# The first sixty microseconds of a retention and GELU kernel: another order of transfers and units, and decay work moved between engines

## The chip, the cores and the metric

The kernel runs on one core of a Trainium2 chip. The metric is the device time of one execution in microseconds, from the first to the last instruction. The engines of a core run side by side, each in the order of its own queue, and wait for one another through semaphores: TensorE (PE in the profile, with its weight loads as PEld), VectorE (DVE), ScalarE (ACT), GpSimd (POOL), and SyncE (SP), which issues most of the transfers.

## The reference

The first part is a retention layer with a decaying state; the second is a feed-forward layer with the quick form of GELU. Everything is float32, but the two weight matrices are handed over as float64 and narrowed in the kernel.

```python
def _attn_ref(q, k, v):                      # (4, 8, 768, 64) each
    gamma = 1.0 - 2.0 ** (-5.0 - np.arange(H))
    scale = 1.0 / np.sqrt(D)
    for t in range(S):
        state = gamma * state + np.einsum('bhd,bhe->bhde', k[:, :, t], v[:, :, t])
        y[:, :, t] = scale * np.einsum('bhd,bhde->bhe', q[:, :, t], state)

def _moe_ref(x, w_in, w_out):                # x (3072, 512), w_in (512, 2048), w_out (2048, 512)
    h = x @ w_in
    g = h * (1.0 / (1.0 + np.exp(-1.702 * h)))
    return g @ w_out
```

Between the two, y is reordered to (B*S, H*D).

## The kernel before

The sequence is cut into 24 chunks: 64 time steps of two batches each. Four chunks make a block of 512 tokens, so there are six blocks. For a chunk j the kernel runs two functions:

- `turn(j)` transposes q and k on TensorE (blocks 0 and 1) into PSUM; ScalarE copies the result to SBUF. `decay(j)` scales k by the column decay.
- `attend(j, f)` makes the scores of chunk j, and, for the chunk f before it, the new state and the output: the product of the old state with q (scaled by the row decay, `rowd`) plus the product of v with the masked scores of f.

```python
    def turn(j):
        ...
            x = QKV.pop(("q", j)), QKV["kn", j]
            p = [ps.tile([P, 2, HP, D], F32, name="pt", tag="y") for i in range(2)]
            ...                      # 64 transposing matmuls against ident
            for i in range(2):
                act.activation(t[:, :, :, HALF[i]], p[i], AF.Copy)          # L229
            decay(j)
        ...
        if j + 2 < NCH and ...: load(j + 2, "qk")

    def decay(j):
        ...
        keep(pool.tensor_mul(KD[j], QKV.pop(("kn", j)), cold[...]))          # L244

    def attend(j, f=None):
        ...                          # scores L252; state L263; old state x q L272; v x scores L278
            dve.tensor_mul(AT[j], pa[:, :, 0], mask)                         # L282
        ...
            if c:
                dve.tensor_mul(tmp, py[:, :, 1]..., rowd...)                 # L293
                dve.tensor_add(x, y, tmp...)                                 # L295
            else:
                act.activation(x, y, AF.Copy)
            if c == 0:
                dve.tensor_copy(new, u)
            elif c < NC - 1:
                pool.tensor_mul(new, old, whole...)                          # L302
                dve.tensor_add(new, new, u)                                  # L303
            if f + 2 < 2 * CB: load(f + 2, "v")
```

`fetch()` issues the load of the next block (512 KB) of w_in, later of w_out, in its float64 form. `narrow()` makes float32 of what has been fetched: one ScalarE instruction and six of VectorE. The first two calls take one block each (together pair 0 of w_in's columns), every further call two blocks (a pair). There are 17 calls.

```python
        tc.keep_in_program_order(act.activation(m, hi, AF.Abs, scale=2.0 ** 16))      # L186
        tc.keep_in_program_order(dve.tensor_scalar(m, m, ..., op0=ALU.min, op1=ALU.max))  # L187
        dve.tensor_scalar(mu, mu, 3, None, op0=ALU.logical_shift_left)                # L189
        dve.scalar_tensor_tensor(hi, hi, 0x80000000, mu, ...)                         # L190
        dve.tensor_scalar(mu, hi, 0xFF800000, None, op0=ALU.bitwise_and)              # L191
        dve.scalar_tensor_tensor(lo, lo, 2.0 ** -52, m, ...)                          # L192
        dve.tensor_add(w, hi, lo)                                                     # L196
        for _ in range(n): fetch()
```

TensorE's order is the order of the text. For the other engines a scheduler orders the instructions when the program is built; `keep_in_program_order` pins an instruction behind the one that stands before it in the text on the same engine.

Block 0 of the feed-forward layer is computed in units `up0(half, p)`: eight matmuls of 256 columns for half of the block's tokens and pair p of w_in's columns, then a sigmoid and a product in `hidden`. Block 1 follows in units `up1(f)`. Then come `down(m)` for each block m, and `up(d)` for the blocks from 2 on; these use seven products of half-size matrices in place of eight, for which sums of w_out's parts (`sums_w2`, `sums_w2_t3`), of w_in's, of x's and of the hidden values (`sums_g`) are made. The start before:

```python
    load(0, "qk"); make_identity(nc, ident)
    ...                              # loads of cold, and of the row decay into m3, spread over 128 partitions
    fetch(); load(0, "v"); fetch(); load(1)
    ...                              # rowd copied out of m3; m3 times cold; selected to a triangle: mask
    keep_warm(7)                     # 7 transposes of ident
    narrow()
    turn(0)
    ...                              # load of whole
    attend(0)
    narrow()
    for _ in range(2): fetch()
    turn(1)
    attend(1, 0)
    for _ in range(2): fetch()
    turn(2)
    for j in range(2, 5):
        attend(j, j - 1)
        turn(j + 1)
        narrow()
        up0(0, j - 2, "x")
    between = [...]                  # (attend(5, 4), turn(6)), (attend(6, 5), turn(7)), attend(7, 6), attend(None, 7)
    for n, unit in enumerate([(1, p) for p in range(3)] + [(half, p) for p in range(3, NP) for half in range(2)]):
        up0(*unit, "xxyx"[n % 4])
        if n % 2 == 0: narrow()
        if n in (1, 4, 7, 10): between.pop(0)()
    for f in range(NFF):
        up1(f)
        if f % 2 == 0: narrow()
        if f >= NFF - 4: sums_w2(2 * (f - NFF + 4))
    ...
        for n, unit in enumerate(down(m)):
            unit()
            if m == 0 and n < NP // 2: sums_w2_t3(2 * n)
```

## Time and profile before

| what | value |
|---|---|
| time, median of three runs | 691.2 us (690.55 to 695.37) |
| span of the profiled run | 692.5 us |
| matmuls of block 0 (`up0`), first and last start | 32.3 and 106.3 us |
| matmuls of block 1 (`up1`), first start | 113.75 us |
| first unit of `down(0)` | 168.8 us |
| moved by the transfers, whole span | 46.85 MB, 68 GB/s |
| moved between 10 and 60 us | 207 to 220 GB/s in each 10 us |

A line of a timeline gives the start in us, the length in us, the engine, the line of the kernel, the operation, the tile written and the tiles read, the shape, the count, and in brackets the idle time of the engine before it and what ended it. A float32 matmul of the text appears as two instructions in the trace. Consecutive matmuls overlap in the profile, so that the time of a group is read from the starts, not from the sum of the single times.

### The profile page before, as it was taken

What the parts mean: (1) busy time and instruction counts of PE and PEld (TensorE: products, weight loads), DVE (VectorE), ACT (ScalarE), POOL (GpSimd) and SP (SyncE); (2) the same over time, 40 slices, a digit from 0 to 9 for tenths busy, and PEclk for the clock granted to TensorE, in tenths of its full rate; (3) what the DMA queues carried; (4) which work ended last, traced back from release to release, by engine and by line L of the source; (5) the groups of instructions that cost most, each with busy time, mean ns of one, the idle gap of its engine ahead of it and who ended that gap; (6) DMA issues with size and microseconds to landing.
All of it is one profiled execution on the core that took longest, in us unless ns stands there. A gap on an engine that the chain in (4) does not pass through costs nothing.

```text
span 692.5 us, 14320 instructions
## 1 busy us (share of the span) xinstructions
PE 670.6 (97%) x6087; PEld 562.0 (81%) x6087; DVE 368.7 (53%) x512; ACT 127.7 (18%) x201; POOL 145.2 (21%) x131
## 2 busy tenths in 40 slices
PE   5779999999999999999999999999999999999997
PEld 4668886445888888888888888888888888888886
DVE  3499999997341563344373445373345373344241
ACT  3232323331000000332000333000233000233000
POOL 4221200000168343100244100244200143000030
PEclk9999999999999999999999999999999999999999
DMA  8875544422212213310323320223320220000001
GB/s 199 220 194 169 160 147 137 168 50 32 41 20 57 66 29 76 74 36 4 68 36 87 74 43 2 58 48 88 74 42 1 45 50 31 17 0 1 16 0 46
DMA packets 140368, 46.85 MB, mean 68 GB/s; under 512 B 131792, under 2 KB 132816, under 8 KB 140304
## 3 DMA queue, kind: packets, MB, share of 16 engines
q1 hardware_dynamic: 136352, 39.10, 24.6%
q0 software_dynamic: 1808, 5.52, 2.2%
q10 hardware_dynamic: 2144, 1.31, 0.6%
q8 instruction: 48, 0.79, 0.5%
q14 instruction: 16, 0.13, 0.1%
HBM read 39.59 MB, written 6.29 MB: 66 GB/s over the span
## 4 chain that ended last, share of the span: by engine, by line
PE 84%; DVE 11%; DMA 3%; issue 1%; POOL 0%; ACT 0%; ACTq 0%; SPq 0%; POOLq 0%
PE pd L439 39%; PE px L386 16%; PE py L386 12%; PE ph L347 8%; PE ph L334 3%; DMA kn_in<-in_k_dram 3%; PE pa L252 2%; PE py L278 1%; PE py L272 1%; DVE W L196 1%; PE pa L263 1%; DMA whole<-in_col_decay_dram 1%; DVE W L189 1%; DVE W L192 1%; DVE W L191 1%
## 5 line engine op out<-in xcount | busy, mean ns | idle before, releaser
L439 PE MATMUL pd<-W,G 128*128 128x256 f32 x1120 | 247.4, 381 | 0.4 <-DVE G L377 0.3
L439 PEld LDWEIGHTS pd<-W,G 128*128 128x128 f32 x1120 | 211.3, 190 | 30.3 <-DVE G L377 1.2
L386 PE MATMUL px<-X,W 128*128 128x256 f32 x512 | 119.0, 379 | 0.0
L386 PEld LDWEIGHTS px<-X,W 128*128 128x128 f32 x512 | 97.3, 190 | 13.2
L386 PE MATMUL py<-X,W 128*128 128x256 f32 x384 | 90.7, 379 | 0.0
L386 PEld LDWEIGHTS py<-X,W 128*128 128x128 f32 x384 | 73.0, 190 | 9.9
L334 PE MATMUL ph<-X,W 128*128 128x256 f32 x256 | 59.8, 394 | 5.9 <-DVE W L196 5.3
L334 PEld LDWEIGHTS ph<-X,W 128*128 128x128 f32 x256 | 50.0, 198 | 13.7 <-DVE W L196 5.5
L244 POOL TENSOR_TENSOR kd<-kn_in,cold 128x512 f32<-128x512 f32 x14 | 17.2, 1225 | 188.1 <-PE pa L263 161.3
L347 PE MATMUL ph<-W,W 128*128 128x512 f32 x128 | 55.2, 593 | 0.3 <-DVE W L315 0.3
L347 PEld LDWEIGHTS ph<-W,W 128*128 128x128 f32 x128 | 24.2, 190 | 30.8 <-issue 29.7
L378 POOL TENSOR_TENSOR G<-G 128x512 f32<-128x512 f32 x20 | 29.5, 1482 | 91.9 <-DVE G L377 90.4
L282 DVE TENSOR_TENSOR at<-pa,mask 128x512 f32<-128x512 f32 x16 | 11.0, 686 | 62.1 <-PE pa L263 53.6
L315 DVE TENSOR_TENSOR G<-G,sg 128x512 f32<-128x512 f32 x48 | 33.0, 688 | 14.0 <-ACT sg L313 14.0
L431 POOL DMA_DIRECT2D out_dram<-o x20 | 14.9, 746 | 121.2 <-DVE o L430 121.2
L313 ACT ACTIVATE sg<-G 128x512 f32<-128x512 f32 x48 | 30.2, 630 | 51.3 <-DVE G L396 30.7
L439 PE MATMUL pd<-W,W 128*128 128x256 f32 x160 | 35.8, 381 | 0.4 <-DVE W L377 0.3
L302 POOL TENSOR_TENSOR state<-state,whole 128x512 f32<-128x512 f32 x20 | 22.0, 1098 | 66.0 <-DVE state L303 60.5
L313 ACT ACTIVATE sg<-ph 128x512 f32<-128x512 f32 x32 | 19.1, 598 | 88.4 <-PE ph L334 40.8
L439 PEld LDWEIGHTS pd<-W,W 128*128 128x128 f32 x160 | 30.2, 190 | 5.6 <-DVE W L377 1.2
L396 DVE TENSOR_TENSOR G<-py,p 128x512 f32<-128x512 f32 x16 | 11.1, 692 | 37.8 <-PE py L386 37.8
L426 ACT ACTIVATE u<-pd 128x512 f32<-128x512 f32 x6 | 3.6, 597 | 135.6 <-PE pd L439 135.6
(105 smaller groups left out, 659.0 us busy)
## 6 DMA issues: line engine op xcount, KB each, us to landing
W<-in_moe_w_in_dram SPq DMA_DIRECT2D x12, 512.0 KB, 5.6
v_in<-in_v_dram SPq DMA_DIRECT2D x48, 128.0 KB, 3.3
kn_in<-in_k_dram SPq DMA_DIRECT2D x42, 128.0 KB, 3.2
W<-in_moe_w_out_dram SPq DMA_DIRECT2D x10, 512.0 KB, 4.1
out_dram<-o POOLq DMA_DIRECT2D x20, 256.0 KB, 2.7
q_sq<-in_q_dram SPq DMA_DIRECT2D x256, 16.0 KB, 1.9
k_sq<-in_k_dram SPq DMA_DIRECT2D x256, 16.0 KB, 1.8
G<-in_moe_w_out_dram SPq DMA_DIRECT2D x6, 512.0 KB, 5.1
```

The source lines that it names most:

```text
L244: keep(pool.tensor_mul(KD[j], QKV.pop(("kn", j)), cold[:, H:2 * H, None].to_broadcast([P, H, D])))
L252: pe.matmul(pa[HALF[i], r, 0, s, :], KT[j][HALF[r], s, HALF[i]], QT[j][HALF[r], s, HALF[i]], start=True, stop=True)
L302: pool.tensor_mul(new, old, whole[:, None, :, None].to_broadcast([P, 2, HP, D]))
L313: act.activation(s, h, AF.Sigmoid, scale=1.702)
L315: dve.tensor_mul(g, h[:, i], s[:, i])
L334: pe.matmul(h[:, ab], w, X[:, 2 * half + c // 2, c % 2, :], start=(ab == 0 and c == 0), stop=(c == 3), skip_group_check=True)
L347: pe.matmul(h, w, X1[:, c // 2:4:2, c % 2, :], start=(c == 0), stop=(c == 3))
L378: pool.tensor_sub(a[1], a[1], a[0])
L386: pe.matmul(acc[:, u, :], W1[:, 2 * d + u, sa, c, :], X[:, sb, c, :], start=(start and u == 0 and c == 0), stop=(stop and c == 1), skip_gr ...
L396: dve.tensor_add(a[0], y, p1)
L431: (pool if m < NB - 1 else act).dma_start(rows[th, e], o)
L439: pe.matmul(p0[:, n, :], g1(m, p, sa)[:, n * P:(n + 1) * P], W2[:, sb, p, :], start=(new and p == 0 and n == 0), stop=(last and p == NP - ...
```

## The change

- **Transfers.** q, k and v of chunk 0 are issued ahead of w_in's first blocks; four blocks are fetched ahead of the units. The row decay is loaded as one row of one partition and spread by a matmul against a row of ones (`rows`).
- **Row decay in q's turn.** In chunks 1 to 7, q is transposed against a diagonal that holds the row decay (`diag`), so that the scores and the product with the old state carry it already. The mask then needs the column decay only. Chunk 0 is turned against the identity, and its output is multiplied by the row decay. For the later chunks the mask gets its row decay during `up1`.
- **ScalarE takes work of blocks 0 and 1.** k's decay becomes eight activations with a scale per partition, the state's decay four; the product with `rowd` becomes a plain copy on ScalarE. Before, GpSimd and VectorE did these.
- **Units.** The first unit of block 0 comes as soon as chunks 0 and 1 are done; the turns of chunks 2 and 3 follow between units. `keep_warm` uses matmuls on quarters of the array in place of transposes, and is called in four places.
- **w_out's sums** move from the end of `up1` to the first product groups of `down(0)`, and the last of them from the first group to the third.

```diff
@@ turn
-                pe.matmul(p[i][HALF[r], n, s, :], x[n][HALF[i], HP * r + s, :], ident[HALF[i], HALF[i]],
+                pe.matmul(p[i][HALF[r], n, s, :], x[n][HALF[i], HP * r + s, :],
+                          ident[HALF[i], HALF[i]] if n or j == 0 else diag[HALF[i], HP * r + s, :],
                           start=True, stop=True)
...
-            decay(j)
+            if j:
+                decay(j)
@@ decay
-        keep(pool.tensor_mul(KD[j], QKV.pop(("kn", j)), cold[:, H:2 * H, None].to_broadcast([P, H, D])))
+        x, d = QKV.pop(("kn", j)), cold[:, H:2 * H, None]
+        if j < 2 * CB:
+            for h in range(H):
+                tc.keep_in_program_order(act.activation(KD[j][:, h], x[:, h], AF.Copy, scale=d[:, h]))
+        else:
+            pool.tensor_mul(KD[j], x, d.to_broadcast([P, H, D]))
@@ attend
+            if c == 0 and f:
+                act.activation(x, y, AF.Copy)
+            elif c == 0:
+                dve.tensor_mul(x, y, rowd[:, :, None, :].to_broadcast([P, HP, 2, D]))
+            else:
+                if f < 2 * CB:
+                    act.activation(tmp, z, AF.Copy)
+                else:
+                    dve.tensor_mul(tmp, z, scale)
                 dve.tensor_add(x, y, tmp.rearrange(by, t=D))
...
-                pool.tensor_mul(new, old, whole[:, None, :, None].to_broadcast([P, 2, HP, D]))
+                if f < 2 * CB:
+                    for s in range(HP):
+                        tc.keep_in_program_order(act.activation(new[:, :, s], old[:, :, s], AF.Copy, scale=whole[:, s:s + 1]))
+                else:
+                    pool.tensor_mul(new, old, whole[:, None, :, None].to_broadcast([P, 2, HP, D]))
                 dve.tensor_add(new, new, u)
@@ start
-    load(0, "qk")
+    load(0, "q")
+    load(0, "k")
+    load(0, "v")
...                                  # cold and row loaded, mask from cold alone
     fetch()
-    load(0, "v")
     fetch()
     load(1)
+    fetch()
+    fetch()
...
-    keep_warm(7)
+    keep_warm(9)
+    turn(0)
+    rd = rows("x")
     narrow()
-    turn(0)
+    attend(0)
...                                  # rowd and diag copied from rd; decay(0); diag selected to a diagonal; whole loaded
-    attend(0)
+    keep_warm(12)
     narrow()
-    for _ in range(2):
-        fetch()
     turn(1)
+    keep_warm(4)
     attend(1, 0)
-    for _ in range(2):
-        fetch()
+    fetch()
+    fetch()
+    keep_warm(4)
+    attend(None, 1)
+    narrow()
+    up0(0, 0, "x")
     turn(2)
-    for j in range(2, 5):
-        attend(j, j - 1)
-        turn(j + 1)
-        narrow()
-        up0(0, j - 2, "x")
-    between = [lambda j=j: (attend(j, j - 1), turn(j + 1)) for j in (5, 6)] + [lambda: attend(7, 6), lambda: attend(None, 7)]
+    up0(0, 1, "x")
+    attend(2)
+    turn(3)
+    narrow()
+    up0(0, 2, "x")
+    attend(3, 2)
+    attend(None, 3)
+    narrow()
+    between = [lambda: turn(4), lambda: (attend(4), turn(5)), lambda: (attend(5, 4), turn(6)),
+               lambda: (attend(6, 5), turn(7)), lambda: attend(7, 6), lambda: attend(None, 7)]
...
-        if n % 2 == 0:
+        if n % 2 == 0 and n < 12:
             narrow()
-        if n in (1, 4, 7, 10):
+        if n in (1, 2, 4, 6, 8, 10):
             between.pop(0)()
@@ up1, down
-        if f >= NFF - 4:
-            sums_w2(2 * (f - NFF + 4))
+        if f == 1:
+            dve.tensor_mul(m3, m3, rows("x"))
...
-            if m == 0 and n < NP // 2:
-                sums_w2_t3(2 * n)
+            if m == 0 and n < NP and n % 2:
+                sums_w2(n - 1)
+            if m == 0 and NP <= n < 3 * NP // 2:
+                sums_w2_t3(2 * (n - NP))
```

More of the change, by code (lines that the diff above doesn't have):

```diff
@@ L96 @@
     rowd = const.tile([P, HP, D], F32, name="rowd")
+    row = G[0:1, 4, 0:2].rearrange("p a (h t) -> p (a h) t", t=D)
+    ones = G[0:1, 4, 2, 0:P]
     cold = const.tile([P, 2 * H], F32, name="cold")
@@ L121, in load @@
                 plain("q", q, "q_sq", 2)
+            if "k" in what:
                 plain("kn", k, "k_sq", 2, sp if j else act)
@@ L242, in decay @@
         KD[j] = home(j, "kd")
-        keep = tc.keep_in_program_order if j == 0 else lambda i: i
-        keep(pool.tensor_mul(KD[j], QKV.pop(("kn", j)), cold[:, H:2 * H, None].to_broadcast([P, H, D])))
+        x, d = QKV.pop(("kn", j)), cold[:, H:2 * H, None]
[4 more added lines that the diff above has]
+            pool.tensor_mul(KD[j], x, d.to_broadcast([P, H, D]))
     def attend(j, f=None):
@@ L289, in attend @@
             by = "p i r (s t) -> p (r s) i t"
-            y = py[:, :, 0].rearrange(by, t=D)
-            if c:
-                tmp = two.tile([P, 2, 2, P], F32, name="tmp", bufs=1)
-                dve.tensor_mul(tmp, py[:, :, 1].rearrange("p r i t -> p i r t"),
-                               rowd.rearrange("p (r s) t -> p r (s t)", r=2)[:, None].to_broadcast([P, 2, 2, P]))
+            y, z = py[:, :, 0].rearrange(by, t=D), py[:, :, 1].rearrange("p r i t -> p i r t")
+            scale = rowd.rearrange("p (r s) t -> p r (s t)", r=2)[:, None].to_broadcast([P, 2, 2, P])
+            tmp = two.tile([P, 2, 2, P], F32, name="tmp", bufs=1)
+            if c == 0 and f:
[7 more added lines that the diff above has]
+                    dve.tensor_mul(tmp, z, scale)
                 dve.tensor_add(x, y, tmp.rearrange(by, t=D))
-            else:
-                act.activation(x, y, AF.Copy)
             u = pa[:, :, 1]
@@ L468, in down @@
         return todo
-    load(0, "qk")
+    load(0, "q")
+    load(0, "k")
+    load(0, "v")
+    W = col_decay.shape[1]
+    for i in range(2):
+        tc.keep_in_program_order(pool.dma_start(
+            cold[HALF[i]].rearrange("p (n h) -> p n h", n=2),
+            bass.AP(tensor=col_decay.tensor, offset=col_decay.offset, ap=[[W, D], [D * W + H, 2], [1, H]])))
+    tc.keep_in_program_order(pool.dma_start(row, row_decay[None, :, 0:D]))
     make_identity(nc, ident)
-    W = col_decay.shape[1]
+    dve.memset(ones, 1.0)
     m3 = mask.rearrange("p r h t -> p (r h) t")
-    for i in range(2):
-        pool.dma_start(cold[HALF[i]].rearrange("p (n h) -> p n h", n=2),
-                       bass.AP(tensor=col_decay.tensor, offset=col_decay.offset, ap=[[W, D], [D * W + H, 2], [1, H]]))
-    pool.dma_start(m3, bass.AP(tensor=row_decay.tensor, offset=row_decay.offset, ap=[[0, P], [P, H], [1, D]]))
     first = const.tile([P, 1], F32, name="first")
@@ L484, with rows @@
     fetch()
-    load(0, "v")
     fetch()
     load(1)
-    idle = ps.tile([P, HP, P], F32, name="idle", tag="x")
+    fetch()
+    fetch()
+    idle = ps.tile([P, 4 * P], F32, name="idle", tag="x")
     def keep_warm(n):
         for _ in range(n):
-            pe.transpose(idle[:, 0, :], ident, ident)
-    for o in range(2):
-        act.activation(rowd[HALF[o]], m3[HALF[o], o:H:2, :], AF.Copy)
-    dve.tensor_mul(m3, m3, cold[:, 0:H, None].to_broadcast([P, H, D]))
+            for h in HALF:
+                pe.matmul(idle[h, 0:P], ident[h, h], ident[h, :], start=True, stop=True)
+    def rows(tag):
+        p = ps.tile([P, H, D], F32, name="rows", tag=tag)
+        pe.matmul(p.rearrange("p h t -> p (h t)"), ones, row.rearrange("p h t -> p (h t)"), start=True, stop=True)
+        return p
+    dve.tensor_copy(m3, cold[:, 0:H, None].to_broadcast([P, H, D]))
     for i in range(2):
-        pool.affine_select(out=m3[HALF[i]], in_=m3[HALF[i]], compare_op=ALU.is_ge, fill=0.0, base=0,
-                           pattern=[[0, H], [1, D]], channel_multiplier=-1)
+        tc.keep_in_program_order(pool.affine_select(
+            out=m3[HALF[i]], in_=m3[HALF[i]], compare_op=ALU.is_ge, fill=0.0, base=0,
+            pattern=[[0, H], [1, D]], channel_multiplier=-1))
+    diag = one.tile([P, H, D], F32, name="diag", tag="kT")
     def chunks(first, last):
@@ L507, in chunks @@
                 for s in (lambda j=j: turn(j), lambda j=j: attend(j, j - 1))]
-    keep_warm(7)
+    keep_warm(9)
+    turn(0)
+    rd = rows("x")
     narrow()
-    turn(0)
+    attend(0)
+    for o in range(2):
+        act.activation(rowd[HALF[o]], rd[HALF[o], o:H:2, :], AF.Copy)
+    act.activation(diag, rd, AF.Copy)
+    decay(0)
+    for i in range(2):
+        tc.keep_in_program_order(pool.affine_select(
+            out=diag[HALF[i]], in_=diag[HALF[i]], compare_op=ALU.is_equal, fill=0.0, base=0,
+            pattern=[[0, H], [1, D]], channel_multiplier=-1))
     for r in range(2):
```

## The prediction

> **What bounds the kernel now.** I read the page first: the busy times and the span in 40 slices.

> ```profile
> span 692.5 us, 14320 instructions
> PE 670.6 (97%) x6087; PEld 562.0 (81%) x6087; DVE 368.7 (53%) x512; ACT 127.7 (18%) x201; POOL 145.2 (21%) x131
> PE   5779999999999999999999999999999999999997
> DVE  3499999997341563344373445373345373344241
> ```

> TensorE (PE) is busy for 670.6 of 692.5 us, so only 21.9 us are idle. The slices say where: the first three, and the last. The stretches view adds up the idle time of PE from 0 to 60 us as 16.5 us, and from 600 us to the end as 4.1 us; in between there are 1.3 us. VectorE (DVE) is as full as PE from slice 3 to slice 9, though only 53% busy over the whole. So a change of the order of work can win something only before about 55 us, and must not push DVE over its limit between 35 and 125 us.

> Next I read the list of waits from 0 to 230 us, for PE.

> ```profile
> PE ph L334 <- DVE W L196: 5.3, 2, 3.4
> PE pa L252 <- ACT G L229: 3.9, 3, 2.8
> PE pt L224 <- DMA q_in<-in_q_dram: 2.9, 2, 2.3
> PE idle L493 <- POOL ident masks.py:199: 2.6, 1, 2.6
> PE pt L224 <- DMA kn_in<-in_k_dram: 1.6, 1, 1.6
> ```

> Columns: total us, times, longest. The waits are of three kinds: for a narrowed block of w_in (L196 is the last DVE instruction of `narrow`), for the copies of the transposed q and k, and for loads. Then the timelines of PE and ScalarE (ACT), first 65 us:

> ```profile
> 30.12 1.06 PE L224 MATMUL pt<-ident,q_in 64*64 64x64 f32 x30 [2.26 <-DMA q_in<-in_q_dram]
> 32.33 4.95 PE L334 MATMUL ph<-X,W 128*128 128x256 f32 x16
> 42.29 3.72 PE L334 MATMUL ph<-X,W 128*128 128x256 f32 x16 [1.88 <-DVE W L196]
> 52.37 9.92 PE L334 MATMUL ph<-X,W 128*128 128x256 f32 x38 [3.39 <-DVE W L196]
> 68.09 10.63 PE L334 MATMUL ph<-X,W 128*128 128x256 f32 x48 [0.68 <-ACT G L229]
> ...
> 32.32 1.08 ACT L229 ACTIVATE G<-pt 128x512 f32<-128x512 f32 x2 [8.19 <-PE pt L224]
> 33.29 1.12 ACT L186 ACTIVATE W<-W 128x1024 f32<-128x1024 f32 x1
> ```

> The three `up0` units of the loop start at 32.33, 42.29 and 52.37 us; **from 52.37 us on PE stands still for no more than 0.7 us at a time** until the tail. The 48 matmuls from 68.09 took 221 ns each, a unit of 16 so 3.54 us. The three units from 52.37 to 64.38 took 12.0 instead of 10.6 us: 1.4 us lost to a lower clock after the 3.39 us wait. The first unit waits for chunk 3's transposes (q lands at 30.1), although it needs only chunks 0 and 1. The two ACT lines show that the `Abs` of a narrow is pinned behind the instruction traced before it: its two blocks of w_in were issued by 19.9 us and no block took over 9.1 us to land, so the pin held it, not the data.

> [...] 1.4 us lost after 3.39 us idle, nothing visible after 1.88 us. [...] Here L189 took 1.42 us beside GpSimd's k decay at 45.2 us and 0.69 at 55.3. [...] here 128x512 from SBUF took 0.67 us and 128x1024 1.15, so about 0.19 us fixed and 0.94 ns per element.

> **The change part by part.**

> (1) Start. The mask needs the column decay only (4 KB a transfer) and no 256 KB row decay, which landed at 10.6 and held ACT and the mask until 13.9. K's second half landed at 8.65 and still sets the end of `turn(0)`, say 9.5. The `Abs` of the first narrow runs about 10.0 to 10.6, 0.9 us earlier than now. From there DVE has no pause: two half narrows of 3.45 us each (0.45+0.45+0.7+0.45+0.7+0.7, the unblocked durations less overlap), two masks, x(0), state, x(1), state at 0.6: 10.5. So DVE is through chunk 1 at about 10.6+10.5 = 21 if nothing is late; the chain through PE and ACT gives 22.4: row decay copies (2 x 0.41), diag 0.6, k's decay in eight strips of 0.19+64x0.00094 = 0.25, together 2.0; the diag's two selects of 0.84 on GpSimd let turn(1) begin at about 13.8; turn 1.0, copies 1.1, attend(1, 0) 2 with the clock up, warm-up 0.9, the last attend 1.5, tmp 0.6, four strips of state at 0.31, add 0.6. **The first unit can start at about 21.5 instead of 32.33.**

> (2) What follows it. The narrow of pair 1 has its `Abs` pinned behind the state strips, so L187 starts at 23.0. A pair costs 0.7+0.7+1.23+0.68+1.23+1.22 = 5.76 us; with one gated product (0.6) in it, pair 1 is ready at 29.4. Unit (0,1) runs 29.4 to 33.0, attend(2) and turn(3) to 34.4, copies to 35.4, k's strips to 37.4, `Abs` to 38.5, pair 2 to 44.3. Unit (0,2) now stands directly behind its own narrow: PE waits from 34.4 to 44.3, goes cold, and needs 3.54+1.7 = 5.2 us, to 49.5. attend(3, 2) to 51.4; tmp, strips, add 2.4; the last attend 0.9, tmp and x 1.2: **unit (1,0) starts at 55.9 and PE is dense from there.**

> (3) Work done by then. Against 52.37 before: one unit more (3.54), turns 4 and 5 (0.94 each) and the scores of chunk 4 (0.5) not yet done: 1.15 us ahead. Equivalent 54.75, against 52.37 plus the 1.4 lost to the clock, 53.8: +1.0 us. To this come the second `rows` product in the dense stretch, 512 columns wide as in L347, where a product is two instructions of 0.43 us: 0.86, and turn(5) right behind a unit that holds a "y" buffer, whose release takes a sigmoid and a product, less 0.5 for the scores between: about 0.7. **Sum +2.6 us.**

> (4) DVE later. Seven tmp products leave (7 x 0.6 = 4.2 us), the twelve subtractions of w_out's sums (12 x 0.6 = 7.2) leave the `up1` stage, and blocks by GpSimd end in chunks 0 to 7. None of it is on the path: PE was dense there. After: the sums have the 14 us of the first two products of `down(0)`, which read slices 0 and 2 of w_out alone. The t3 subtractions (4 x 0.6) fall beside sums_g, where PE waited 0.29 us at 196.3; DVE was idle for 8.45 us before 180, and will probably do them early. Worth: 0.

> **Rivals.** A, the sum above: the wait for the narrows only moves, from 42 and 52 to 29 and 34 us. For it: the pins, and DVE's 5.76 us a pair, which nothing shortens. It gives 691.2+2.6 = 693.8. B: the whole chain starts earlier than I put it, since q, k and v now stand ahead of w_in's blocks in the queue (k, 2 us earlier), the strips overlap on ACT (1 us each in the two chains that count, 2 us), turn(5) finds its buffer (0.7), and the third unit's wait is filled or short enough for the clock to stay up (1.7). Against A that is 6.4: 687.4. For it: ACT's two copies from PSUM take 1.08 where one takes 0.6, so they overlap, and the warm-up counts (12 and 4) look like values tuned against this very gap. Against it: rowd's two copies did not overlap (0.84 for two of 0.41). C: the loads bound it. The stretches show 207 to 220 GB/s between 10 and 60 us; by unit (0,1) q and k of chunks 0 to 2, v of 0 and 1 and four to six blocks of w_in are needed, 4.2 to 5.2 MB, that is 20 to 25 us at 210 GB/s, less than the 29.4 of DVE. If GpSimd's later transfers or a full queue delay them, 4 us more than A: 697.8.

> **Range and chances.** A takes the late end of nearly every estimate, so I weigh A 0.3, B 0.6 and C 0.1: 0.3x693.8 + 0.6x687.4 + 0.1x697.8 = 690.4. I put **690.0 us**, a range of 684.0 to 696.0. Two per cent is 13.8 us, near the whole idle time before 55 us, so faster by that has 0.06, slower 0.03, within 0.91.

> **What would show it.** Unit (0,0) at 20 to 23 us; PE idle before (0,1) and, longest of all, 8 to 10 us before (0,2), ended by the last instruction of a narrow; a granted clock below 1 in the slice after; from (1,0) on no wait over 1.5 us; DVE below 98% between 60 and 125 us; no GpSimd decay before `down(0)`; the end of `up1` within 3 us of 169. I am wrong if the third unit starts before 40 us (then B and more), if a load ends PE's waits after 20 us (C), or if the time from the first `down` unit to the end is not the old 523.7 us within 1 us.

## The result: the change makes the kernel slower, and the profile after

| kernel | median us | before, same chip | ratio with 95% interval |
|---|---|---|---|
| after | 709.87 (709.66 to 711.66) | 691.36 | 1.0259 [1.0223, 1.0296] |

The prediction was 690.0 us with a range up to 696.0: it was wrong. All rivals named in it lay below 698 us as well.

The first part of the page of the kernel after: busy times, two engines in 40 slices, and the clock granted to TensorE.

```profile
span 708.0 us, 14607 instructions
PE 675.6 (95%) x6200; PEld 564.6 (80%) x6200; DVE 364.2 (51%) x508; ACT 154.4 (22%) x300; POOL 127.6 (18%) x118
PE   7647999999999999999999999999999999999997
DVE  3634988799671183344383344383344383344241
PEclk9967999999999999999999999999999999999999
```

Where the kernel before had "577" in PE's first three slices and nines from the fourth, there is now "7647". A slice is 17.7 us, so the third and fourth are 35 to 71 us: there PE is less busy, and its clock is down to six and seven tenths. From the fifth slice on PE is full again. The loss lies in the stretch that was to become shorter.

The list of waits of the kernel after, first 230 us, PE alone (total us, times, longest):

```profile
PE ph L354 <- DVE W L199: 12.9, 2, 10.1
PE idle L519 <- POOL ident masks.py:199: 3.9, 1, 3.9
PE ph L354 <- DVE X L313: 2.9, 2, 1.4
PE pa L274 <- issue: 2.6, 1, 2.6
PE py L289 <- issue: 1.7, 1, 1.7
```

L354 is the matmul of `up0`, L199 the last VectorE instruction of `narrow` (L334 and L196 before). The wait for the narrows grew from 5.3 to 12.9 us, 10.1 of it in one piece. No load stands in these lines any more; before, q and k made up 4.5 us. "issue" in the last two lines is PE standing still without a releaser that the list knows; it comes up again below.

PE's timeline of the kernel after. In order: the units (0,0), (0,1), (0,2), the last scores and state of chunk 3, the units (1,0) and (1,1), and the first `up1`.

```profile
24.34 1.56 PE L354 MATMUL ph<-X,W 128*128 128x256 f32 x6 [1.44 <-DVE X L313]
...
32.40 5.38 PE L354 MATMUL ph<-X,W 128*128 128x256 f32 x16 [2.81 <-DVE W L199]
...
49.42 5.95 PE L354 MATMUL ph<-X,W 128*128 128x256 f32 x16 [10.09 <-DVE W L199]
...
60.04 0.69 PE L274 MATMUL pa<-v_in,G 64*64 64x64 f32 x32 [2.65 <-issue]
63.72 9.09 PE L354 MATMUL ph<-X,W 128*128 128x256 f32 x32 [1.42 <-DVE X L313]
...
127.64 7.13 PE L367 MATMUL ph<-W,W 128*128 128x512 f32 x16 [1.37 <-DVE W L335]
```

The first unit starts 8 us earlier than before (24.34 against 32.33), as intended, and (0,1) and (0,2) still start earlier than they did (42.29 and 52.37 before). The fourth, (1,0), is late: the point from which PE is dense came at 52.37 us before and comes at 63.72 now, with 1.15 us of work more done. `up1` starts at 127.64 against 113.75, 13.9 us late; `down(0)` starts at 183.92 against 168.79, 15.1 late; and from there to the end of the span it is 524.1 us against 523.7. That makes 15.5 us between the two spans, not 18.5: the profiled execution of the kernel before took 694.2 us, 2.8 more than its median.

What stands behind the wait of 10.09 us: the timelines of ScalarE and then of VectorE in the kernel after.

```profile
39.42 1.08 ACT L234 ACTIVATE G<-pt 128x512 f32<-128x512 f32 x2 [1.02 <-PE pt L228]
40.40 2.01 ACT L253 ACTIVATE G<-kn_in,cold 128x64 f32<-128x64 f32 x8
42.30 1.10 ACT L189 ACTIVATE W<-G 128x1024 f32<-128x1024 f32 x1
```

```profile
43.44 0.69 DVE L190 TENSOR_SCALAR W<-W 128x1024 f32<-128x1024 f32 x1 [3.71 <-ACT W L189]
...
48.14 1.23 DVE L199 TENSOR_TENSOR W<-G 128x1024 f32<-128x1024 f32 x1
```

ScalarE copies the turned q and k of chunk 3, then scales k in eight strips (2.01 us), and only then does the `Abs` (L189) that opens the narrow of pair 2. VectorE had nothing to do for 3.71 us, then works 5.9 us on the pair while PE stands still.

### The profile page after: what moved, and what is told of

The parts are those of the page before. It is cut to its first block, busy times and chain, and to the rows that moved or that the text cites. A ratio compares the mean times of both kernels' runs of the same rounds, so it can differ in the third digit from the quotient of the medians.

```text
span 708.0 us, 14607 instructions
## 1 busy us (share of the span) xinstructions
PE 675.6 (95%) x6200; PEld 564.6 (80%) x6200; DVE 364.2 (51%) x508; ACT 154.4 (22%) x300; POOL 127.6 (18%) x118
## 4 chain that ended last, share of the span: by engine, by line
PE 89%; DVE 7%; ACT 2%; issue 2%; POOL 0%; ACTq 0%; POOLq 0%
PE pd L459 39%; PE px L406 16%; PE py L406 12%; PE ph L367 8%; PE ph L354 6%; PE pa L263 2%; PE py L289 2%; PE py L283 1%; PE pa L274 1%; PE pt L228 1%; PE idle L519 1%; ACT W L189 1%; DVE W L199 1%; DVE G L396 1%; DVE W L396 1%
## 5 line engine op out<-in xcount | busy, mean ns | idle before, releaser
L354 PE MATMUL ph<-X,W 128*128 128x256 f32 x256 | 63.9, 410 | 16.7 <-DVE W L199 12.9
L354 PEld LDWEIGHTS ph<-X,W 128*128 128x128 f32 x256 | 51.9, 206 | 25.7 <-DVE W L199 10.2
L398 POOL TENSOR_TENSOR G<-G 128x512 f32<-128x512 f32 x20 | 29.5, 1482 | 91.8 <-DVE G L397 91.8
L322 POOL TENSOR_TENSOR state<-state,whole 128x512 f32<-128x512 f32 x13 | 14.3, 1098 | 122.0 <-DVE state L323 121.7
```

The lines of the kernel that those rows point to most:

```text
L322: pool.tensor_mul(new, old, whole[:, None, :, None].to_broadcast([P, 2, HP, D]))
L354: pe.matmul(h[:, ab], w, X[:, 2 * half + c // 2, c % 2, :], start=(ab == 0 and c == 0), stop=(c == 3), skip_group_check=True)
L398: pool.tensor_sub(a[1], a[1], a[0])
```

## The experiments

My theory after the comparison: the order of the text ties the narrow of pair 2 behind `turn(3)` and its strips, and the units right behind it; the wait and the cold clock after it (0.50 from 43.74 to 53.98 us) are the loss, and ScalarE's strips make it longer. Its rival: not the order but the other parts (transfers, row decay, work on ScalarE) are the loss. A third theory, that PE waits for its own instructions, came up with e4. The quoted expectations were each written before their run, and some give the theories letters: O is the order, S ScalarE's strips, F the wait for instructions.

All medians are in us; "over" is the difference to the median of the kernel before on the same chip.

| run | median | before | over | ratio with 95% interval |
|---|---|---|---|---|
| after | 709.87 | 691.36 | +18.5 | 1.0259 [1.0223, 1.0296] |
| e1: decays back on GpSimd | 701.98 | 693.17 | +8.8 | 1.0114 [1.0037, 1.0192] |
| e2: narrow of pair 2 early | 697.80 | 693.17 | +4.6 | 1.0058 [1.0037, 1.0080] |
| e3: before, new order of units only | 714.84 | 693.17 | +21.7 | 1.0297 [1.0233, 1.0361] |
| e4: after, old order of units | 711.92 | 693.17 | +18.8 | 1.0247 [1.0181, 1.0313] |
| e5: e4, eight warm-up rounds more | 705.14 | 692.99 | +12.2 | 1.0171 [1.0117, 1.0224] |
| e6: e1 and e2 together | 696.47 | 692.99 | +3.5 | 1.0053 [1.0035, 1.0071] |
| e7: before, sums moved only | 694.21 | 692.99 | +1.2 | 1.0008 [0.9986, 1.0030] |
| e8: e5 with decays on GpSimd | 701.39 | 692.99 | +8.4 | 1.0125 [1.0069, 1.0182] |
| e9: before, narrow a line up | 693.14 | 694.39 | -1.3 | 0.9985 [0.9965, 1.0006] |
| e10: e9, unit ahead of the turn too | 694.26 | 694.39 | -0.1 | 0.9998 [0.9982, 1.0015] |
| e11: before, 48 idle matmuls more | 699.84 | 694.39 | +5.5 | 1.0070 [1.0047, 1.0094] |
| e12: e3 with narrow of pair 2 early | 705.55 | 694.39 | +11.2 | 1.0133 [1.0079, 1.0186] |
| e13: after, warm-up ahead of (0,2) | 710.40 | 693.67 | +16.7 | 1.0253 [1.0190, 1.0315] |
| e14: before, new transfers only | 697.36 | 693.67 | +3.7 | 1.0054 [1.0036, 1.0073] |

In the first row the kernel before has the median of four executions, in the others of 23 to 55 on other chips; against those medians 709.87 is 15.5 to 16.9 us over.

### e2: the narrow one step earlier

```diff
     up0(0, 0, "x")
+    narrow()
     turn(2)
     up0(0, 1, "x")
     attend(2)
     turn(3)
-    narrow()
     up0(0, 2, "x")
```

> The changed kernel with one line moved: the narrow of pair 2 is traced directly behind the first unit, not behind turn(3). Theory O: VectorE goes from pair 1 to pair 2 without its pause of 11 us; pair 2 is ready near 38.5 us instead of 49.4, the third unit starts near 40 us, the clock stays up, unit (1,0) starts near 52 instead of 63.7 us, and the time falls by 11 to 14 us, to 696 to 699. Theory S: the strips still stand in the chain; under 4 us gained, about 707.

This moves one line. The `Abs` of pair 2 is now pinned ahead of the copies and strips of chunks 2 and 3. PE's timeline of this kernel, units (0,1), (0,2) and (1,0):

```profile
33.07 5.16 PE L354 MATMUL ph<-X,W 128*128 128x256 f32 x16 [3.67 <-DVE W L199]
39.72 3.72 PE L354 MATMUL ph<-X,W 128*128 128x256 f32 x16
...
51.17 7.17 PE L354 MATMUL ph<-X,W 128*128 128x256 f32 x32 [1.43 <-DVE X L313]
```

The wait of 10.09 us is gone, the unit (0,2) runs warm (3.72 us), and the dense stretch starts at 51.17 instead of 63.72. Of the 18.5 us over, 4.6 are left: **a tie between two lines of text is worth 13.9 us** (12.1 if the two medians are compared as they stand, 709.87 and 697.80). This is the clearest single result, and a hit. Part of it is the clock: the waits ahead of the last attend and of (1,0) are the same as in the kernel after (2.65 and 1.43 us), but the units behind them took 7.17 us and not 9.09; step (2) below says why.

### e1 and e6: the decays back on GpSimd

```diff
-        if j < 2 * CB:
-            for h in range(H):
-                tc.keep_in_program_order(act.activation(KD[j][:, h], x[:, h], AF.Copy, scale=d[:, h]))
-        else:
-            pool.tensor_mul(KD[j], x, d.to_broadcast([P, H, D]))
+        pool.tensor_mul(KD[j], x, d.to_broadcast([P, H, D]))
...                                  # and the same for the state's four strips
```

> The changed kernel with k's and the state's decay of blocks 0 and 1 back on GpSimd, unpinned; the copy of the old state's product stays on ScalarE, the order of units too. Theory O (the third unit stands directly behind its own narrow; ScalarE's strips only lengthen the chain): the Abs of pair 1 comes 1.0 us earlier (no state strips, 1.26), that of pair 2 another 2.0 us (no k strips), the last attend of chunk 3 another 1.3 us; the third unit starts near 46.4 instead of 49.4 us and the time falls by 4 to 6 us, to about 705. Theory S (the strips and their pins are the loss): most of the 18.5 us comes back, below 697.

PE's timeline of e1, the unit (0,2) and the last scores and state of chunk 3:

```profile
46.39 6.44 PE L345 MATMUL ph<-X,W 128*128 128x256 f32 x16 [8.20 <-DVE W L199]
...
55.63 0.69 PE L269 MATMUL pa<-v_in,G 64*64 64x64 f32 x32 [0.78 <-DVE state L314]
```

The time of unit (0,2) came as expected; the gain, 9.7 us (7.9 between the medians as they stand), is larger. Here too the clock has a part, for unit (0,1) took 3.69 us and (1,0) with (1,1) 7.17. Beside the strips that stand ahead of the narrow there is a second place: the wait before the last attend fell from 2.65 to 0.78 us. In the kernel after the state's four strips are pinned behind the copy `tmp`, and that waits for the end of the attend. ScalarE and VectorE of the kernel after, at that place:

```profile
57.47 0.60 ACT L310 ACTIVATE tmp<-py 128x512 f32<-128x512 f32 x1 [1.46 <-PE py L289]
57.96 1.26 ACT L320 ACTIVATE state<-state,whole 128x128 f32<-128x128 f32 x4
```

```profile
59.26 0.69 DVE L323 TENSOR_TENSOR state<-state,pa 128x512 f32<-128x512 f32 x1 [0.47 <-ACT state L320]
```

The decay of the old state needs nothing of this attend, and GpSimd does it long before (at 24.20 us in e1). On ScalarE it comes in the order of the text, behind `tmp`, and VectorE's add of the new state ends 0.6 + 1.26 + 0.69 us behind the last matmul. PE waits for it at 60.04 us, since the add reads the one PSUM tile `pa`, which the next attend writes. The bracket there says "issue": the list did not find this releaser, but the VectorE line ends at 59.95, and in e1 the list names it.

Both repairs together, e6:

> The changed kernel with both repairs: pair 2 narrowed early and k's and the state's decay back on GpSimd. If the two losses add (12 and 8 us alone): 689 to 692, level with before or 0.5% faster. If they overlap, as both shorten the same wait of the third unit: 693 to 696, most of the gain from the early narrow, of GpSimd only 2 to 4 us at the last attend of chunk 3.

It came to +3.5, half a microsecond above the range put for repairs that overlap. They do overlap: on top of e2 the decays are worth 1.1 us and not 9.7, because with the early narrow the strips have nothing urgent behind them.

### e3, e12: the order of units by itself

e3 is the kernel before with nothing but the new sequence of turns, attends, narrows and units; its start then reads as in the diff of the change. e12 has the line of e2 in it, too.

> The kernel before with the changed kernel's order of units and nothing else: no strips, no diag, its old transfers, mask and sums. Theory O: the order alone makes the loss; first unit near 29.5 us, third near 49 to 50, the time 703 to 708. Theory S, or a loss by the row decay or the transfers: within 3 us of before, 688 to 694.

> The kernel before with the changed kernel's order of units, as tried, but pair 2 narrowed early; no other part of the change. Theory O: 12 to 15 us better than the order alone (714.8), so 699 to 703. Against the mended changed kernel with GpSimd decays (696.5) it tells what the other parts, transfers, row decay and warm-up, are worth in the new order: about 4 us if the early start of chunk 1 (the unit at 24.5 instead of 27.2 us) carries through, 0 if not.

PE's timeline of e3, units (0,1), (0,2), and (1,0):

```profile
38.23 6.55 PE L334 MATMUL ph<-X,W 128*128 128x256 f32 x16 [4.70 <-DVE W L196]
...
54.54 5.23 PE L334 MATMUL ph<-X,W 128*128 128x256 f32 x16 [8.21 <-DVE W L196]
...
69.62 9.67 PE L334 MATMUL ph<-X,W 128*128 128x256 f32 x32 [4.35 <-DVE X L295]
```

The order alone loses 21.7 us, more than I expected and more than the whole change. All three waits that it makes are there. The early narrow (e12) takes 10.5 of this back, less than the 12 to 15 expected, which leaves +11.2 where e6 has +3.5: so in the new order the parts that e12 lacks (transfers, row decay in q's turn, plain copy, warm-up) are together worth some 7.7 us. One place where they help is the chain to x, which PE waits for here (L295, 4.35 us; 1.42 in the kernel after); which of them does it was not tried. The parts of the change belong together, and their sum still doesn't pay.

### e4, e5, e8: everything but the order, and a new kind of wait

```diff
-    attend(None, 1)
-    narrow()
-    up0(0, 0, "x")
...
+    for j in range(2, 5):
+        attend(j, j - 1)
+        turn(j + 1)
+        narrow()
+        up0(0, j - 2, "x")           # the old loop, and the old list of what lies between
```

> The changed kernel with the order of units of before (attend, turn, narrow, unit, so that each unit runs one narrow ahead of the pair it waits for), all else as changed. Theory O: near before, 689 to 695; of the rest of the change the strips cost 1 to 3 us, the freed VectorE and the missing 256 KB give some back. Theory S: over 700.

If the order were the whole loss, this should have been no slower than the kernel before. It was 18.8 us over: a miss, and at first sight it speaks for the rival. The list of waits of e4 says something else:

```profile
PE pt L228 <- issue: 7.9, 4, 3.4
PE ph L354 <- DVE W L199: 7.4, 2, 4.5
...
PE py L289 <- issue: 2.1, 1, 2.1
...
PE pa L274 <- issue: 1.4, 1, 1.4
```

PE stood still 11.4 us in six pieces (7.9 + 2.1 + 1.4) for nothing that a semaphore explains, each in the middle of a run of equal small matmuls. Two of them on PE's timeline:

```profile
32.00 0.69 PE L228 MATMUL pt<-ident,kn_in 64*64 64x64 f32 x11 [1.82 <-issue]
...
77.09 1.12 PE L228 MATMUL pt<-ident,kn_in 64*64 64x64 f32 x30 [3.37 <-issue]
```

From each of the six to the next there are 127, 128, 380, 256 and 255 matmuls of the trace, about one to three times 128. Each pause ends 1.25 to 1.47 us after the end of one 16 KB packet of the queue whose kind the profile calls "instruction". One of these packets (the transfers view of e4, 72 to 78 us: packets, MB, share):

```profile
q8 instruction: 1, 0.02, 1.3%
```

Each matmul of the trace has its weight load (the page of the kernel after counts 6200 of either), so 128 matmuls are 256 instructions of PE. The number of packets is near that: in the kernel after, this queue moved 48 of them, 0.79 MB, for those 12400 instructions, one to 258. I call 256 instructions a block and the place between two blocks a border, a reading of these counts; where a pause lay at a border in e4, it cost up to 3.4 us. This gave the new theory, F: PE waits for its own instructions where it goes through small matmuls quickly while transfers are dense. If so, moving all later instructions by a few places must move the pauses or end them; if the parts of the change are slow by themselves, more warm-up can only make it slower.

```diff
-    keep_warm(12)
+    keep_warm(20)                    # in e4: 16 matmuls more of the text, which move all later instructions by 64 places
```

> The changed kernel with the old order of units, as in the run before, but 20 warm-up pairs in place of 12 ahead of turn(1). This shifts all later TensorE instructions by 64 places and costs 1.7 us of warm-up. Theory F (in the old order the time is lost while TensorE waits for its own instructions: six pauses of 1.4 to 3.4 us stood at every 127 or 128 matmuls, each next to a 16 KB packet of the instruction queue; a pause comes where two such borders lie inside one run of small matmuls): with the borders moved most pauses go, and 711.9 us fall to 695 to 701. Theory S (ScalarE's strips cost the time there): 1 to 2 us slower than 711.9, since the warm-up is longer.

The pauses fell from 11.4 to 4.5 us, and the time by 6.6 us, though PE does more. That speaks for F, but 705.14 us is not the 695 to 701 that I expected. The rest of e5 was tested by taking the strips back too (e8):

> The changed kernel with the old order of units, the decays on GpSimd and the shifted borders: what is left of the change is the order of the first transfers, the row decay in q's turn, the copy on ScalarE, the warm-up and the sums. Theory O: these are worth little, 689 to 695, no further from before than 4 us. If the row decay in q's turn itself costs (diag on GpSimd ahead of turn(1), one more matmul in up1): 696 to 700.

It is still 8.4 us over, outside both ranges. The transfers alone cost 3.7 us (e14, below); the other 4.7 are row decay, copy and pauses (5.4 us in this profile), which I did not take apart.

### e11: the pauses on the kernel before itself

```diff
+    for n in range(48):              # ahead of attend(0): moves PE's later instructions by 192 places
+        pe.matmul(idle[HALF[n % 2], 0, 0:D], ident[HALF[n % 2], HALF[n % 2]], ident[HALF[n % 2], HALF[n % 2]],
+                  start=True, stop=True)
```

> The kernel before with 48 idle matmuls of 64 columns ahead of attend(0), where TensorE waits 2.8 us anyway. They move the borders of the instruction blocks by 192 places, to where the old-order run of the changed kernel had them; nothing else is different. Theory F: pauses without a visible cause appear in the runs of small matmuls, up to 10 us together, and the time rises by 4 to 12 us, to 696 to 704. If those pauses were due to something else in the changed kernel (its strips, its loads): within 1.5 us of before.

A hit, +5.5 us, for idle matmuls that lie in time that PE spends waiting. The list of waits of e11, where the kernel before has no line with "issue" at all:

```profile
PE pt L224 <- issue: 4.1, 4, 1.4
PE pa L263 <- issue: 3.8, 1, 3.8
PE py L278 <- issue: 0.9, 2, 0.6
```

Where such a pause lies matters as for any wait. The longest, 3.77 us at 28.41, cost nothing: the first unit started at 32.63 and the third at 51.87, about as before. Two in the dense stretch, of 1.43 us at 68.10 and 0.89 at 83.72, are most of the 2.6 us by which `up1` started later (116.34 against 113.75). The profiled execution took 696.82 us, 3.0 less than the median of e11, so the rest of the 5.5 us is not in this profile. So where the borders of the instruction blocks fall can be part of what an edit of this start does to the time, here up to 5.5 us.

### e14: the new order of transfers by itself

```diff
-    load(0, "qk")
+    load(0, "qkv")
...
     fetch()
-    load(0, "v")
     fetch()
     load(1)
+    fetch()
+    fetch()
...                                  # the two fetches after the second narrow removed
```

> The kernel before with the change's order of the first transfers and nothing else: v of chunk 0 ahead of w_in's first blocks, four blocks ahead of the units. If this order costs: q and k of chunks 2 and 3 land 3 to 5 us later, the first unit starts near 36 us, the time rises by 3 to 5 us to 696 to 699. If not: within 1.5 us of before.

PE's timeline of e14, `turn(2)`:

```profile
24.41 1.36 PE L224 MATMUL pt<-ident,q_in 64*64 64x64 f32 x30 [4.08 <-DMA q_in<-in_q_dram]
```

Two blocks of w_in more (1 MB) now stand ahead of q of chunk 2 in the queue, and PE waits 4.08 us for it. The third unit still starts at 52.71, near the old 52.37, but this and the next two units take 13.42 us in place of 12.07, and `up1` starts 1.7 us later. The time is 3.7 us up. How it comes to that is not shown: in this profile the wait ahead of the third unit is as long as before (3.33 and 3.39 us), and most of the 1.7 us is a clock that stayed at half for 6.83 us instead of 3.41.

### e7, e9, e10, e13: no effect, and two misses

e7 moves w_out's sums in the kernel before as the change does.

> The kernel before with only the sums of w_out moved into down(0), as the change does. All theories: VectorE was idle there and TensorE dense, so within 1 us of before. If the last subtractions fall between those of the hidden values, the wait of 0.3 us at 196 grows to 2 us: at most 2 us slower.

The interval holds 1: neutral, as step (4) said. e9 and e10 were tries at a faster kernel: in the old loop the narrow goes a line up, ahead of `turn(j + 1)`, and in e10 the unit too.

> The kernel before with narrow() one line up in its loop, ahead of turn(j+1), so that the Abs is no longer pinned behind the copies that wait for the next chunk's load. The instruction stream of TensorE is the same. Theory O (what counts is when a narrow can begin): pair 1 begins near 29.5 instead of 34.5 us, the second unit no longer waits, the third starts near 47 instead of 52.4 us with the clock up; 684 to 688. If the loads bound the start (theory C of the prediction): 690 to 693.

> As the run before, and each unit ahead of turn(j+1) as well, so the first unit starts as soon as chunks 0 and 1 are done, near 29.5 us, which is the sensible half of the change's order. Theory O: another 1 us, 683 to 688. The stream of TensorE is permuted, so theory F allows a pause or two of 1 to 3 us that were not there: then 686 to 691.

Neither gained. PE's timeline of e9, first two units:

```profile
33.73 6.75 PE L334 MATMUL ph<-X,W 128*128 128x256 f32 x16 [2.01 <-DVE X L295]
...
45.87 4.98 PE L334 MATMUL ph<-X,W 128*128 128x256 f32 x14 [1.79 <-issue]
```

The second and third unit no longer waited for a narrow (1.88 and 3.39 us before). But VectorE now did the narrow ahead of x, so the first unit came 1.4 us later, and at half clock it took 1.8 us longer; and two matmuls into the second unit PE paused for 1.79 us. This kernel has the same sequence of PE instructions as the kernel before and shows pauses at "issue" which that one's profile doesn't: in these two kernels the place in PE's sequence alone does not decide on a pause. e13 puts 32 rounds of warm-up (128 matmuls of the trace, so 256 instructions, a whole block, and the borders stay) into the 10.09 us wait of the kernel after.

> The changed kernel with 32 warm-up pairs ahead of the third unit, in its wait of 10 us. They are 256 instructions, so the borders of the instruction blocks stay where they were; at full clock they take 6.8 us. If the clock after the wait is a loss of its own: the third unit takes 3.6 instead of 5.95 us and the next two 7.1 instead of 9.0, and the time falls by 3 to 5 us, to 705 to 707. If the clock is only the shadow of the wait: within 1.5 us of 709.9.

PE's timeline of e13, the warm-up and the unit (0,2):

```profile
39.84 7.17 PE L519 MATMUL idle<-ident 64*64 64x128 f32 x128
...
50.23 5.38 PE L354 MATMUL ph<-X,W 128*128 128x256 f32 x16 [3.23 <-DVE W L199]
```

The warm-up ended 3.23 us too early: the unit took 5.38 us, a little less than 5.95, but not 3.6. So this run does not separate the clock from the wait; the record of the clock does better, in step (2) below.

## Why the prediction was wrong

**Sum and weights.** The mechanism of rival A was right, the wait for the narrows only moved; rival B, which got 0.6, was wrong in all four of its items. "A takes the late end of nearly every estimate" is the sentence that failed: A was too early at each stage. In A itself the step that failed most is (2), by its cost of the cold clock: 1.7 us put, 6.7 measured. The late start of step (1) adds 2.8. The stages, in us:

| stage | prediction | measured | late by | what the step lacked |
|---|---|---|---|---|
| unit (0,0) | 21.5 | 24.34 | 2.8 | copies of chunk 1 done at 17.01 for 15.9; a pause of 1.72 at "issue" in attend(1, 0), from 18.55 on |
| unit (0,1) | 29.4 | 32.40 | 3.0 | nothing more: one pair after the other, as put |
| unit (0,2) | 44.3 | 49.42 | 5.1 | unit (0,1) cold after 2.81 us: 5.38 in place of 3.6 |
| unit (1,0) | 55.9 | 63.72 | 7.8 | unit (0,2) 5.95 in place of 5.2; last attend 2.3 in place of 0.9, of which 0.5 because its three products take 1.4 at full clock |
| start of `up1`, over before | 1.7 | 13.9 | 12.2 | the 7.8 above; units (1,0) and (1,1) cold, 9.09 in place of 7.17; wait of 1.37 ahead of `up1` (0.26 before); 1.03 in place of 0.7 for the "y" buffer; about 1 us not assigned |

The 1.7 of the last line is the +1.0 of step (3) and the 0.7 for the "y" buffer.

**Step (1), the start.** Its durations held: k's strips took 2.01 us for the 2.0 put, the state's 1.26 for 4 x 0.31. The items of its chain add up to 22.7 us and not to 22.4, and to the 21.5 that it puts if the state's strips are left out, on which x does not wait. The chain was late by 1.1 us at the copies of chunk 1, and no pause of PE was in it; how much of the 1.72 us counts is open, since the product with the old state had to wait for VectorE until 20.66 us in any case. VectorE's instructions beside GpSimd's, 1.42 us for 0.69 in the prediction's example (L189, one tile read), were slower in the kernel after, too: L195, which reads two tiles, took 1.03 us at 14.27 beside GpSimd's select of `diag`, and 0.69 at 18.04.

**Step (2), what follows.** The order of events was as written: the `Abs` behind the strips, a pair of 5.9 us (5.76 put), PE waiting "8 to 10 us before (0,2)" (10.09), ended by the narrow's last instruction. The mis-sized term is the clock. The step took one cold unit, (0,2), and said that PE is dense and warm from (1,0) on; in fact the clock was at half in three stretches, which reach into (0,1), (0,2), and the last attend with (1,0) (busy PE, PEld, DVE, ACT and POOL with counts, then the granted clock, the transfers' share, GB/s):

```profile
33.50:36.91 3.41, 3.41 (x9) 2.71 (x9) 0.00 (x0) 0.00 (x0) 0.00 (x0) 0.50 0.94 320
43.74:53.98 10.24, 4.56 (x11) 3.62 (x12) 5.46 (x6) 0.00 (x0) 0.00 (x0) 0.50 0.44 133
60.80:67.63 6.83, 5.41 (x69) 4.51 (x61) 3.78 (x5) 2.79 (x6) 0.00 (x0) 0.50 0.23 51
```

The matmuls of unit (0,2) start 427 ns apart at half clock, up to 53.85 us, and 215 ns apart behind it. PE worked 3.41 + 4.56 + 5.41 us at half clock, and I put the loss at half of that, 6.7 us, where step (2) had 1.7 (half of the 3.41 us that the clock stays at 0.50 in the kernel before, from 31.45 and again from 51.93): 1.7 in (0,1), 2.3 in (0,2), 2.7 in the last attend and (1,0). From the 1.88 us wait of the kernel before, with no loss visible behind it, I took waits below 3 us to be free, an estimate that the runs don't bear out. Between 10 and 100 us of all 16 profiles the clock changes only at the borders of steps of 3.41 us, and where these steps lie differs from run to run. A step at half clock was the last one where PE was busy for 86% or more of it, and was followed by another where PE was busy for 81% or less; a step at full clock was followed by half only where PE was busy for at most 51% of it (and not always then). So in these runs a wait counted by how it lay in the steps. The wait of 2.65 us that begins at 57.39 falls into one step, and two steps at half clock follow. In e2 the same wait lies across a border (46.30), and PE is at full clock behind it. A wait of 2.04 us in e8 was followed by a unit of 5.41 us, one of 2.74 in e1 by a unit of 3.69.

**Step (3), work done by then.** The 1.15 us of work ahead were right. The "y" buffer's 0.7 was a wait of 1.03 us, put down to the `Abs` of a narrow (L189); the 0.68 ahead of the unit before it are in the kernel before as well. `rows` took 1.05 us for the 0.86. Not in the step: the wait of 1.37 us ahead of `up1`.

**Step (4)** held: the sums are worth nothing (e7), and from the first `down` unit to the end it is 524.1 us for the 523.7 put.

**Rival C** (loads bound it) is half right. No load ends a wait of PE in the kernel after, but the new order of transfers costs 3.7 us on the kernel before (e14); the prediction took it for harmless.

**What B overlooked.** B let "the strips overlap on ACT" and the third unit's wait be filled. The strips overlapped no further than put (2.01 us for eight), and nothing filled the third unit's wait: PE did no work in those 10.09 us, and what follows the unit in the text ran behind it. Moving one `narrow()` (e2) would have been the thing to ask for: the prediction wrote down that unit (0,2) "now stands directly behind its own narrow" and did not weigh it.

**Sum of the +18.5 us.** With the early narrow 4.6 are left, so the tie accounts for 13.9, the lost clock included; with GpSimd's decays as well 3.5 (e6). Those 3.5 have the size of what the transfers cost in e14; but the `rows` product (1.05) and the wait ahead of `up1` (1.1 more than before) lie in them too, so the parts don't add up neatly, and I leave the last 3.5 us undivided. None of the versions was clearly faster than the kernel before.

## What to carry to other kernels

When an order is pinned on several engines, write down for every pinned instruction what stands ahead of it on its engine: a helper whose first step waits behind another chunk's copies is late by all of them, and the engine behind it is late and then, as PE here from 49.42 to 53.98 us, at half clock. Work that depends on nothing near belongs on an idle engine with a queue of its own: the state's decay was early on GpSimd (24.20 us in e1), on ScalarE it sat behind a copy (57.96 us in the kernel after). Move the narrow or load up first, the consumer second, and count the low clock behind every wait (6.7 us here, by the estimate above), not only in the next unit: no length of wait came out of these runs below which it is sure to be free.

## What the runs showed of the hardware that I had not expected

```profile
66.68:68.09 1.41, 0.00 (x0) 0.00 (x0) 1.41 (x2) 0.00 (x0) 0.29 (x1) 1.00 0.00 0
```

Pauses also differ between kernels with the same PE stream (1.79 us in e9 where the list of the kernel before has none). Single executions of the kernel before lie between 689 and 699 us, and this spread goes with the granted clock: of 139, the 16 with a mean clock of 0.998 or more have a median of 690.8 us, the 16 with 0.987 or less one of 695.7. Whether pauses or the place of the clock's steps make that difference was not tried.
